# Adaptive layer norm, attention and MLP on one core: priorities varied by kind and time, gates folded into weights, q placed by DMA, two head groups moved

## The chip, the core and the metric

One core of a Trainium2 chip runs the whole program. The metric is device time in microseconds (us), the median over several executions. A profile is one execution taken by the hardware profiler; its span runs from the first to the last instruction. Engines: PE (matrix multiply, with PEld for its weight loads), DVE (VectorE), ACT (ScalarE), POOL (GpSimd), SP (issues DMAs).

## The reference

A transformer block on x of 2048 rows by 512 columns. Six vectors (shift, scale and gate for two branches) come from a conditioning vector c. Cut to what matters:

```python
mod = silu(c) @ w_mod                       # 512 -> 6 x 512: sa, ca, ga, sb, cb, gb
h = layernorm(x) * (1 + ca) + sa
q, k, v = split(h @ wqkv)                   # 32 heads of 16 columns
o = softmax(q @ k.T / 4) @ v                # per head, 2048 x 2048 scores
x = x + ga * (o @ wo)
h = layernorm(x) * (1 + cb) + sb
x = x + gb * (gelu(h @ w1 + b1) @ w2 + b2)  # inner width 1376
```

All tensors are bfloat16. The gates ga and gb are one value per output column.

## The kernel before, in words

**Tiles.** Rows are handled in four blocks b of 512 queries. The 32 heads are four groups cc of eight; a group's q and k lie in 128 partitions, so that four heads (one of each pair, picked by a parity) are multiplied at once in four 32-row strips of PE. A "run" is one block, one group and one parity: 32 runs of 16 key tiles of 128 keys. A score tile is one strip's 128 keys by 512 queries; there are 32 x 16 x 4 = 2048. For the last block a run is both parities and half of the queries.

**q.** `make_q` projects q of a block and group into PSUM and writes the tile `qm` with two halves, one per parity: q scaled, with the rows of the other parity set to zero by the mask `qmask` (L701), so that the 32-row strip's matmul adds only the wanted head of the pair.

**Exponentials on two engines.** Three or two score tiles at a time go to PSUM (`st`) and ACT takes their exponential to `pt` (L840). Of each run up to four key tiles (2, 6, 10, 14) are shared: DVE takes the exponential instead, by an integer trick: one `ph` (L881) per score tile and, for a whole key tile, four shifted copies `sh` (L896), all five summed on PE with weighted copies `VX` of v. If DVE is behind, ACT takes shared tiles as well (`next_tile`, `d_run`). L791 are the score matmuls, L929 the products with v into `od`.

**Normalisation.** At a run's end DVE copies `od` (L954). SP sends the sums to DRAM and back (`dn`, `dc`), DVE inverts them (L965), SP spreads them (`rn`, `RB`), POOL multiplies (L981), and for every second run SP moves the odd heads' rows into place (L991).

**Tails.** `block_tail` follows a block's last run: Wo (L1079), times the gate ga (L1129), plus x (L1131), layer norm, W1 (L1148), bias (L1158), gelu on ACT (L1167), W2 (L1085), times the gate gb (L1180), plus the residual (L1183), out. Its pieces are spread over the next runs. The last block is done in two halves: the first by `block_tail` with two row tiles, the second by `last_half` (L1232, L1237, L1240, L1268, L1271, L1284, L1287), when no scores are left. Of the first half's eleven W1 tiles `PSUM_F` = 4 are taken out by DVE early; the others wait for PSUM that the scores free.

**What sets the order.** The kernel writes its order itself. Each piece of work is an `Op` with an engine, an estimated duration, what it depends on and a priority; `Plan` steps through an estimated time and picks on each engine the ready operation of the lowest priority number (`pick`, `dyn`, `commit`). What it picks is emitted in that order. On the chip every engine takes its instructions in order and waits on semaphores where data is not there. `heat` inserts matmuls without use to keep PE's clock up. All DMAs but one stand in SP's queue. The first loads are, in order: two halves of x's first block, two blocks of w_mod, three 128-column parts of wqkv, then the other blocks of x and the rest of wqkv.

**Order of runs.** `runs` goes block by block, group by group, parity by parity. k and v of a later group are made with a due time before its first run (`due`, `urgent`).

Of the kernel before, what the change touches and what calls it, by code (L numbers as in the profile page):

```python
# [59 lines left out]
FILL = 1.6  # L60
HEAT = 1.3
# [41 lines left out]
class Plan:  # L103
# [39 lines left out]
    def pick(self, eng):  # L143
        can = [(self.start(o), o) for o in self.lists[eng] if o.gate is None or o.gate()]
        can = [(s, o) for s, o in can if s < 1e17]
        if not can:
            return None
        if eng == "PE":
            can = self.ahead(can)
        first = min(s for s, _ in can)  # L150
        near = [(self.dyn(self, o), s, o.seq, o) for s, o in can if s <= first + self.SLACK[eng]]
        _, s, _, o = min(near)
        return s, o

# [22 lines left out]
    def commit(self, s, o):  # L177
# [36 lines left out]
        if o.kb:  # L214
            q = "SP"
            self.bus[q] = max(self.bus[q], s + o.us + 0.9) + o.kb / (310.0 if s < 12.0 else 260.0)
            o.end = self.bus[q] + 0.7
# [33 lines left out]
def kernel(  # L251
# [15 lines left out]
    P = 128  # L267
# [23 lines left out]
    PSUM_F = 4  # L291
# [29 lines left out]
    r_qm = res("qm", 4, [P, 2, QB], BF16)  # L321
# [4 lines left out]
    r_y = res("y", 2, [P, D], BF16)  # L326
# [165 lines left out]
    for h in range(2):  # L492
# [3 lines left out]
    o_wm = {i: dma(lambda o, i=i: nc.sync.dma_start(out=o.tile, in_=wm_src[:, :, i * D:(i + 1) * D]),  # L496
                   kb=512, acq=r_blk, prio=0.01 + 0.01 * i) for i in (0, 1)}
# [4 lines left out]
    def load_cols(i, lo, hi, prio):  # L502
        return dma(lambda o: nc.sync.dma_start(out=o_w[i].tile[:, :, lo:hi],
                                               in_=wq_src[:, :, i * D + lo:i * D + hi]), (o_w[i],),
                   kb=hi - lo, prio=prio)
    o_w0 = {i: load_cols(i, 0, P, 0.1 + 0.01 * i) for i in range(3)}
    o_w1 = {}
    for b in range(1, NQ):
        o_x[b] = load_x(b)
        o_x[b].prio = 0.2 + 0.1 * b  # L510
        o_w1[b - 1] = load_cols((1, 2, 0)[b - 1], P, D, 0.25 + 0.1 * b)
# [16 lines left out]
    o_mask = op("DVE", mask, 0.4, (o_io,), prio=0.0)  # L528
# [163 lines left out]

    def make_q(b, cc, kind, acq):
        qm = op("NIL", None, 0.0, (), lat=0.0, prio=0.0, acq=r_qm)
        mm = proj(b, o_w[0], cc, kind, acq, after=qm)
        if (b, cc) == (0, 0):
            evs = [op("DVE", lambda o, p=p: nc.vector.tensor_scalar(
                out=qm.tile[:, p, :], in0=mm.tile[:, 0:QB], scalar1=qmask[:, p:p + 1], scalar2=None,
                op0=ALU.mult), 0.6, (mm, qm, o_mask), prio=0.1 if p == 0 else 0.45, rel=(mm,)) for p in range(2)]
        else:  # L700
            evs = 2 * [op("DVE", lambda o: nc.vector.tensor_tensor(  # L701
                out=qm.tile, in0=mm.tile[:, 0:QB].unsqueeze(1).to_broadcast([P, 2, QB]),
                in1=qmask.unsqueeze(2).to_broadcast([P, 2, QB]), op=ALU.mult), 1.14, (mm, qm, o_mask),
                prio=0.3, rel=(mm,))]
        o_q[(cc, b)] = (qm, evs)
        qm.uses += 1
        q_left[(cc, b)] = 8 * NT
# [31 lines left out]
    runs = [(b, u) for b in range(NQ) for u in range(8)]  # L739
# [260 lines left out]

    def beside(fn, deps, rel=(), prio=0.5):

        return [op("POOL", lambda o, c=c: after_dve(fn(slice(c * HB, (c + 1) * HB))), POOL_US, deps, lat=0.1,
                   prio=prio, kind="beside", rel=rel, port=True, gate=lambda: plan.beside(POOL_MIN))
                for c in range(2)]
# [66 lines left out]
    def residual(o, ps, gate_t, dst, base, y):  # L1072
        nc.vector.tensor_tensor(out=y, in0=ps, in1=gate_t, op=ALU.mult)
        nc.vector.tensor_tensor(out=dst, in0=y, in1=base, op=ALU.add)

# [39 lines left out]
    def block_tail(b, nt=TPB):  # L1115
# [8 lines left out]
        for t in range(nt):  # L1124
            a = chain([(lambda ps, t=t, u=u: wo_mm(ps, b, t, u, u + 1), MM) for u in range(NC)],
                      [x for u in ots for x in u.two] + [prev], kind, r_ax, ots, 2)
            prev = a
            y = op("NIL", None, 0.0, (a, x2, o_late["ga"]), lat=0.0, prio=0.0, acq=r_y)
            m = op("DVE", lambda o, t=t, a=a, y=y: nc.vector.tensor_tensor(  # L1129
                out=y.tile, in0=a.tile, in1=ga_bc, op=ALU.mult), 0.6, (y,), prio=0.1, rel=(a,))  # L1130
            res_done.append(op("DVE", lambda o, t=t, y=y: nc.vector.tensor_tensor(  # L1131
                out=x2.tile[:, t, :], in0=y.tile, in1=xr.tile[:, t, :], op=ALU.add), 0.33,
                (m, xr), prio=1.5, rel=(y,), port=True))
# [40 lines left out]
        for t in range(nt):  # L1174
# [4 lines left out]
            y = op("NIL", None, 0.0, (mm,), lat=0.0, prio=0.0, acq=r_y)  # L1179
            m = op("DVE", lambda o, mm=mm, y=y: nc.vector.tensor_tensor(  # L1180
                out=y.tile, in0=mm.tile, in1=gb_bc, op=ALU.mult), 0.6, (y,), prio=3.0 if part else 0.1,
                rel=(mm,))
            a = op("DVE", lambda o, t=t, y=y: nc.vector.tensor_tensor(  # L1183
                out=o.tile, in0=y.tile, in1=x2.tile[:, t, :], op=ALU.add), 0.33,
                (m, o_late["gb"]), prio=3.0 if part else 1.5, acq=r_o, rel=(y, x2), port=True)
# [6 lines left out]
    def last_half():  # L1192
# [17 lines left out]
        for n, t in enumerate(tiles):  # L1210
# [18 lines left out]
            def wo2(o, t=t):  # L1229
# [6 lines left out]
            y = take(r_y, (w, x2))  # L1236
            m = op("DVE", lambda o, t=t, y=y: nc.vector.tensor_tensor(  # L1237
                out=y.tile, in0=acc[t].tile, in1=ga_bc, op=ALU.mult), 0.62, (y,), prio=0.024 + n / 50,
                rel=(acc[t],))
            a = op("DVE", lambda o, t=t, y=y: nc.vector.tensor_tensor(  # L1240
                out=x2.tile[:, t, :], in0=y.tile, in1=xr.tile[:, t, :], op=ALU.add), 0.34,
                (m, xr), prio=0.023 + n / 50, rel=(y,))
# [32 lines left out]
            for f in range(NF):  # L1275
# [7 lines left out]
            y = take(r_y, (prev,))  # L1283
            m = op("DVE", lambda o, first=first, y=y: nc.vector.tensor_tensor(  # L1284
                out=y.tile, in0=first.tile, in1=gb_bc, op=ALU.mult), 0.66, (y,), prio=0.1,
                rel=(first,))
            a = op("DVE", lambda o, t=t, y=y: nc.vector.tensor_tensor(  # L1287
                out=o.tile, in0=y.tile, in1=x2.tile[:, t, :], op=ALU.add), 0.34, (m,), prio=0.1,
                acq=r_o, rel=(y,))
# [7 lines left out]
    for b in range(NQ):  # L1297
# [14 lines left out]
        make_v(b, 0, kind, r_ax, "DVE")  # L1312
    for cc in range(1, NC):
        due(32 + APR * (2 * cc - 1) - CB, CB * 0.7 / 8)
# [12 lines left out]
    def want_q(g):  # L1327
        while q_made[0] < g and q_made[0] + 1 < NQ * NC:
            q_made[0] += 1
            b, cc = divmod(q_made[0], NC)  # L1330
# [3 lines left out]
            if cc == NC - 1:  # L1334
                o_h[b].uses -= 1
                if b == NQ - 1:
                    o_w[0].uses -= 1
# [4 lines left out]
    while True:  # L1342
# [7 lines left out]
        while ended:  # L1350
# [4 lines left out]
            for cc in range(1, NC):  # L1355
                if r >= 2 * cc - 3:
                    urgent.add(f"c{cc}")
                    urgent.add(f"in{cc}")
# [4 lines left out]
            if r == 0:  # L1363
                late_loads(o_last[0])
                o_late["ga"] = gate_bc(ga_bc, o_late[2], "gate")
                lt = {3: o_late[3], 4: o_late[4]}
# [16 lines left out]
            if r == 6:  # L1383
# [3 lines left out]
                o_late["w2"] = W2[1]  # L1387
# [39 lines left out]
```

## Time and profile before

| what | us |
|---|---|
| median of 6 runs | 790.29 (788.9 to 791.76) |
| profiled execution | 790.98 |
| its span | 789.2 |
| first exponential starts | 15.48 |
| last exponential ends | 763.7 |
| mean of one exponential, three tiles / two | 1.528 / 1.103 |

The granted TensorE clock is 0.997 over the span. A group's line in the profile reads: line, engine, operation, out<-in with shapes, count, then busy time and the mean ns of one, then the idle time of the engine just before them and what ended it. Durations overlap: an engine starts the next instruction before the last has quite ended, so a sum of durations is above the busy time. In the chain of waits each line is start, length, what.

### The profile page before, as it was taken

Reading aid. Unit: us, or ns where it says so; the run is one execution under the profiler, and the core shown is the slowest. Engines: PE = TensorE matmul, PEld = TensorE weight load, DVE = VectorE, ACT = ScalarE, POOL = GpSimd, SP = SyncE. Lnnn points to the kernel's source line nnn. Section 1 sums busy time; section 2 is a strip of 40 time slices with the busy share of each in tenths; the row PEclk is TensorE's granted clock in tenths of the full one; section 3 lists DMA queues with packets and bytes.
Section 4 is the critical chain, followed back from the end, with each engine's and each line's share of the span. In section 5 each row is a group of like instructions: output and inputs, shape, how many; then the busy total and the mean of one; then the engine's idle time right before and its main releaser. Section 6 shows DMA issues by size and latency. Waiting matters only on the chain.

```text
span 789.2 us, 20172 instructions
## 1 busy us (share of the span) xinstructions
PE 731.2 (93%) x8167; PEld 273.4 (35%) x8249; DVE 742.0 (94%) x1297; ACT 760.6 (96%) x690; POOL 99.0 (13%) x239
## 2 busy tenths in 40 slices
PE   8899999998999999999999999999999999999997
PEld 3433323332323322222322322232233443434444
DVE  6879799999999999999999999999999999999974
ACT  4999999999999999999999999999999999999993
POOL 5622303200001101010001000000000110010000
PEclk9999999999999999999999999999999999999999
DMA  7214000102100000001100000001100001000010
GB/s 214 81 61 107 19 16 19 44 8 68 43 19 15 20 15 20 16 9 31 50 20 16 17 19 2 19 29 30 45 17 20 5 18 44 19 24 15 27 44 27
DMA packets 35231, 26.22 MB, mean 33 GB/s; under 512 B 16037, under 2 KB 30534, under 8 KB 35138
## 3 DMA queue, kind: packets, MB, share of 16 engines
q1 hardware_dynamic: 35130, 24.94, 11.2%
q8 instruction: 64, 1.05, 0.5%
q14 instruction: 29, 0.24, 0.1%
q10 hardware_dynamic: 8, 0.00, 0.0%
HBM read 21.30 MB, written 2.61 MB: 30 GB/s over the span
## 4 chain that ended last, share of the span: by engine, by line
ACT 36%; PE 30%; DVE 19%; issue 11%; DMA 3%; SPq 0%; POOLq 0%; DVEq 0%; POOL 0%; ACTq 0%
ACT pt L840 36%; PE od L929 10%; PE st L791 8%; DVE ph L881 7%; DVE sh L896 6%; PE ax L1085 3%; PE ax L791 2%; PE ax L1148 2%; PE ax L682 1%; DVE g L1158 1%; DVE qm L701 1%; DMA dn<-OD 1%; DMA blk<-in_w_mod_dram 1%; DMA dc<-dn 1%; DVE OD L954 1%
## 5 line engine op out<-in xcount | busy, mean ns | idle before, releaser
L840 ACT ACTIVATE pt<-st 128x1536 bf16<-128x1536 f32 x632 | 718.0, 1316 | 3.7 <-PE st L791 1.9
L881 DVE TENSOR_SCALAR ph<-ax 128x512 int16<-128x512 f32 x468 | 306.6, 685 | 12.4 <-PE ax L791 11.1
L896 DVE TENSOR_SCALAR sh<-ph 128x2048 int16<-128x2048 int16 x468 | 304.6, 693 | 1.4 <-PE od L929 0.9
L791 PE MATMUL st<-qm,kT 32*128 32x512 bf16 x1580 | 247.6, 383 | 27.6 <-ACT pt L840 22.8
L929 PE MATMUL od<-sh,VX 128*32 128x512 bf16 (+1 forms) x2352 | 166.5, 341 | 7.2 <-DVE sh L896 6.2
L791 PE MATMUL ax<-qm,kT 32*128 32x512 bf16 x468 | 162.9, 379 | 4.7 <-DVE ph L881 3.7
L791 PEld LDWEIGHTS <-kT 32*128 32x128 bf16 x2048 | 82.7, 91 | 240.5 <-issue 230.7
L929 PE MATMUL od<-pt,VEB 128*32 128x512 bf16 (+1 forms) x1972 | 147.4, 340 | 0.7 <-ACT pt L840 0.4
L929 PEld LDWEIGHTS <-VEB 128*32 128x32 bf16 x2560 | 62.4, 96 | 78.5 <-issue 66.0
L929 PEld LDWEIGHTS <-VX 128*32 128x32 bf16 x2352 | 58.7, 95 | 87.2 <-issue 75.7
L981 POOL TENSOR_TENSOR OT<-OD,RB 128x256 bf16<-128x256 f32 x38 | 27.5, 736 | 284.3 <-DVE sh L896 189.7
L929 PE MATMUL od<-ph,VEB 128*32 128x512 bf16 (+1 forms) x588 | 46.5, 339 | 1.1 <-DVE OD L954 0.9
L981 POOL TENSOR_TENSOR OS<-OD,RB 128x256 bf16<-128x256 f32 x24 | 17.2, 727 | 187.3 <-DVE sh L896 166.0
L1148 PE MATMUL ax<-blk,W 128*128 128x512 bf16 (+1 forms) x128 | 36.8, 369 | 1.5 <-issue 0.5
L682 PE MATMUL ax<-blk,w 128*128 128x512 bf16 x96 | 33.0, 390 | 3.8 <-DVE blk L607 1.2
L728 POOL TENSOR_SCALAR VX<-VEB 128x128 bf16<-128x128 bf16 x64 | 23.5, 367 | 56.2 <-DVE VEB L614 52.4
L1085 PE MATMUL ax<-w,g 128*128 128x512 bf16 x101 | 28.6, 381 | 0.7 <-issue 0.2
L1158 DVE TENSOR_SCALAR g<-ax,b1c 128x512 bf16<-128x512 f32 (+1 forms) x37 | 26.6, 718 | 0.1
L588 DVE BATCH_NORM_STATS2 ln_s<-xb 128x6 f32<-128x512 bf16 x32 | 21.8, 680 | 1.9 <-DMA xb<-in_A_x_dram 1.8
L954 DVE COPY OD<-od 128x512 f32<-128x512 f32 x31 | 21.3, 686 | 2.4 <-PE od L929 1.6
L1085 PEld LDWEIGHTS <-g 128*128 128x128 bf16 x176 | 14.2, 97 | 21.3 <-issue 11.0
L1148 PEld LDWEIGHTS <-W 128*128 128x128 bf16 x176 | 13.9, 97 | 20.4 <-issue 14.0
(109 smaller groups left out, 364.6 us busy)
## 6 DMA issues: line engine op xcount, KB each, us to landing
RB<-rn SPq DMA_DIRECT2D x124, 64.0 KB
xb<-in_A_x_dram SPq DMA_DIRECT2D x8, 512.0 KB
out_dram<-o SPq DMA_DIRECT2D x16, 128.0 KB
W<-in_B_w_dram SPq DMA_DIRECT2D x1, 1376.0 KB
w<-in_A_wqkv_dram SPq DMA_DIRECT2D x3, 384.0 KB
blk<-in_w_mod_dram SPq DMA_DIRECT2D x2, 512.0 KB
g<-in_w_mod_dram SPq DMA_DIRECT2D x2, 512.0 KB
xb<-in_w_mod_dram SPq DMA_DIRECT2D x2, 512.0 KB
```

The lines of the kernel that those rows point to most:

```text
L682: return chain([(lambda ps, j=j: nc.tensor.matmul(out=ps[:, 0:QB], lhsT=w.tile[:, j, cc * P:(cc + 1) * P], rhs=o_h[b].tile[:, j, :], start ...
L728: nc.gpsimd.tensor_scalar(out=v_cols(VX[(t, ph)])[:, 8 * cc:8 * cc + 8, 0:16], in0=v_cols(v_tile(t, 0))[:, 8 * cc:8 * cc + 8, 0:16], scala ...
L791: nc.tensor.matmul(out=o.tile[:, k * QB:(k + 1) * QB], lhsT=kT[cc][kb][rows, ko * P:(ko + 1) * P], rhs=qm.tile[rows, par, :] if hb is None ...
L840: nc.scalar.activation(out=e.tile[:, 0:len(got) * QB], in_=o.tile[:, 0:len(got) * QB], func=ACT.Exp, scale=ESC)
L881: nc.vector.tensor_scalar(out=ph.tile[:, o.row * QB:(o.row + 1) * QB], in0=o.tile, scalar1=PH_B, scalar2=0.0, op0=ALU.add, op1=ALU.max)
L896: sh = op("DVE", lambda o, j=j: nc.vector.tensor_scalar(out=o.tile, in0=first.tile, scalar1=PH_SH[j], scalar2=None, op0=ALU.add), 0.6, es, ...
L929: nc.tensor.matmul(out=o_od[r].tile[32 * i:32 * i + 32, n * HB:n * HB + w], lhsT=v_tile(kt, ph)[:, c0:c0 + 32], rhs=got[i][:, at:at + w], ...
L954: OD = op("DVE", lambda o: nc.vector.tensor_copy(out=o.tile, in_=od.tile), 0.6, (last,), prio=0.0, acq=r_OD, rel=(od,))
L981: two = beside(lambda c: nc.gpsimd.tensor_tensor(out=OT.tile[:, c], in0=OD.tile[:, c], in1=o5.tile[:, c], op=ALU.mult), (OT,), (OD, o5))
L1085: nc.tensor.matmul(out=ps, lhsT=g[:, f, col:col + P], rhs=rhs, start=(f == 0), stop=(f == NF - 1))
L1148: mm = chain([(lambda ps, f=f, j=j: nc.tensor.matmul(out=ps[:, 0:N], lhsT=W1[:, j, f * P:(f + 1) * P], rhs=h.tile[:, j, 0:N], start=(j == ...
L1158: ev.append(op("DVE", lambda o, f=f, mm=mm: nc.vector.tensor_scalar(out=g.tile[:, f, 0:N], in0=mm.tile[:, 0:N], scalar1=b1c[:, f:f + 1], s ...
```

## The change

- `Plan.pick` adds to every operation's priority a term from 0 to 0.15 (`SPREAD`), a hash of the operation's kind and of a seed; there are 32 seeds, one for each 25 us of planned time.
- The gates are multiplied into weights once, on POOL: ga into Wo and WoP, gb into W2 and W2c (`scaled`, `w2_scaled`; W2c's last row tile holds b2 as well). So the residual of a tile is one DVE operation (PSUM plus x) in place of two (PSUM times gate, plus x). The tile `y` goes.
- q, but for the first group: DVE writes a scaled copy `qs`, and eight DMAs of 16 partitions by 512 columns place its rows in `qm`, whose other rows POOL has zeroed once, at the start.
- Order of runs: after block 0 group 0 come block 1 group 0, block 0 group 1, block 1 group 1, then the rest block by block; the due times of k and v of the later groups follow (`wait`).
- `PSUM_F` goes from 4 to 8: in the first half of the last block DVE takes out eight W1 tiles early, and three are left.
- The first load of wqkv waits until the first block of w_mod has landed (`behind`). Some estimates of durations change.

The instructions that come out differ by these counts: 476 `ph` and 476 `sh` (468 before); 314 exponentials of three tiles and 315 of two (316 each); 15 `qs` for 15 `qm` products; 32 residual operations for 64; 34 more POOL products, six more POOL memsets; 120 more DMAs on SP.

```diff
+SPREAD = 0.15
+SEEDS = (571, 338, 517, 702, ...)
...
-        near = [(self.dyn(self, o), s, o.seq, o) for s, o in can if s <= first + self.SLACK[eng]]
+        near = [(self.dyn(self, o) + self.spread(o), s, o.seq, o) for s, o in can if s <= first + self.SLACK[eng]]
...
+    def spread(self, o):
+        x = ((sum(map(ord, o.kind)) if o.eng == "PE" else o.fn.__code__.co_firstlineno if o.fn else 0) * 2654435761 ^ SEEDS[min(int(self.now // 25.0), len(SEEDS) - 1)] * 2246822519) & 0xFFFFFFFF
+        x = ((x ^ x >> 15) * 2246822519) & 0xFFFFFFFF
+        return SPREAD * ((x ^ x >> 13) & 1023) / 1024.0
...
-    PSUM_F = 4
+    PSUM_F = 8
...
+    QM = [keep.tile([P, 2, QB], BF16, name=f"qm{n}") for n in range(4)]
...
+    def behind(i, load):
+        tc.add_manual_dep(load.ins, first[i].ins.name, mybir.DependencyInfo(
+            mybir.DependencyClass.Sync, mybir.DependencyReason.DATA), reason="order of loads")
...
+            got = nc.sync.dma_start(out=o_w[i].tile[:, :, lo:hi], in_=wq_src[:, :, i * D + lo:i * D + hi])
+            if lo == 0 and i == 0:
+                behind(0, got)
...
+    o_qz = [op("POOL", lambda o, n=n, p=p: nc.gpsimd.memset(QM[n][:, p, :], 0.0), 0.5, prio=0.5 + n)
+            for n in range(1, 4) for p in range(2)]
...
-            evs = 2 * [op("DVE", lambda o: nc.vector.tensor_tensor(
-                out=qm.tile, in0=mm.tile[:, 0:QB].unsqueeze(1).to_broadcast([P, 2, QB]),
-                in1=qmask.unsqueeze(2).to_broadcast([P, 2, QB]), op=ALU.mult), 1.14, (mm, qm, o_mask),
-                prio=0.3, rel=(mm,))]
+            qs = op("DVE", lambda o: nc.vector.tensor_scalar(
+                out=o.tile, in0=mm.tile[:, 0:QB], scalar1=QSC, scalar2=None, op0=ALU.mult), 0.6, (mm, qm),
+                prio=0.3, acq=r_qs, rel=(mm,))
+
+            evs = []
+            for p in range(2):
+                rows = [dma(lambda o, at=slice(i, i + 16), p=p: nc.sync.dma_start(
+                    out=qm.tile[at, p, :], in_=qs.tile[at, :]), [qs] + o_qz, kb=16, n=1.4, prio=0.4 + p, rel=(qs,))
+                    for i in range(16 * p, P, 32)]
+                evs.append(op("NIL", None, 0.0, rows, lat=0.0, prio=0.0))
...
-    runs = [(b, u) for b in range(NQ) for u in range(8)]
+    early = [(1, 0),(0, 1),(1, 1)]
+    groups = [(0, 0)] + early + [(b, cc) for b in range(NQ) for cc in range(NC) if (b, cc) not in [(0, 0)] + early]
+    runs = [(b, 2 * cc + p) for b, cc in groups[:LAST * NC] for p in range(2)] + [(LAST, u) for u in range(8)]
+    wait = {cc: 2 * groups.index((0, cc)) for cc in range(NC)}
...
+    def scaled(parts, gate_t, deps):
+        got = []
+        for w in parts:
+            got += beside(lambda c, w=w: nc.gpsimd.tensor_tensor(
+                out=w()[:, c], in0=w()[:, c], in1=gate_t[:, c], op=ALU.mult), deps, prio=2.0)
+        return op("NIL", None, 0.0, got, lat=0.0, prio=0.0)
...
-            m = op("DVE", lambda o, t=t, a=a, y=y: nc.vector.tensor_tensor(
-                out=y.tile, in0=a.tile, in1=ga_bc, op=ALU.mult), 0.6, (y,), prio=0.1, rel=(a,))
-            res_done.append(op("DVE", lambda o, t=t, y=y: nc.vector.tensor_tensor(
-                out=x2.tile[:, t, :], in0=y.tile, in1=xr.tile[:, t, :], op=ALU.add), 0.33,
-                (m, xr), prio=1.5, rel=(y,), port=True))
+            res_done.append(op("DVE", lambda o, t=t, a=a: nc.vector.tensor_tensor(
+                out=x2.tile[:, t, :], in0=a.tile, in1=xr.tile[:, t, :], op=ALU.add), 0.6,
+                (a, xr), prio=0.1, rel=(a,)))
```

The other three residuals (`block_tail`'s output, both of `last_half`) change in the same way.

## The prediction

> **What bounds the kernel now.** I read the page's busy shares first, then the busy time by stretch, then who waits for whom inside the long stretch, then the chain of waits for the pace of the exponentials, and last the timeline of the first 16 and the last 25 us.
>
> ```profile
> PE 731.2 (93%) x8167; PEld 273.4 (35%) x8249; DVE 742.0 (94%) x1297; ACT 760.6 (96%) x690; POOL 99.0 (13%) x239
> ```
> ```profile
> 0.00:28.00 28.00, 23.15 (x187) 10.81 (x189) 20.87 (x52) 15.12 (x18) 15.14 (x66) 1.00 0.68 207
> 28.00:764.00 736.00, 687.38 (x7809) 249.16 (x7882) 708.24 (x1216) 733.10 (x638) 82.22 (x170) 1.00 0.10 26
> 764.00:789.20 25.20, 20.64 (x181) 13.44 (x178) 12.90 (x30) 12.39 (x36) 1.60 (x4) 0.98 0.14 43
> ```
> The columns behind the stretch's length are PE, PEld, DVE, ACT, POOL. Three engines look nearly full, but from 28 to 764 us only ACT is: 733.1 of 736.0 us, 2.9 us idle, while DVE has 27.8 and PE 48.6 us of idle time. Before 28 us ACT works 15.1 us of 28; behind 764 us half. So there are three stages: a head (until the exponentials run without gaps), a body that lasts as long as ACT's queue of exponentials, and a tail (last query rows through the MLP). What ACT waits for in the body is little:
> ```profile
> ACT pt L840 <- PE ax L791: 1.1, 3, 0.8
> ACT pt L840 <- PE st L791: 0.9, 4, 0.4
> ACT pt L840 <- PE od L929: 0.3, 1, 0.3
> ```
> The pace of ACT is in the chain of waits (start, length, what):
> ```profile
> 84.39 1.21 ACT pt L840
> ...
> 86.62 1.14 ACT pt L840
> ...
> 88.85 1.14 ACT pt L840
> ```
> A pair of exponentials (three score tiles of 512 columns, then two) starts every 2.23 us: 0.446 us a tile. Starts at 82.14, 83.47, 84.39 split that into 1.33 and 0.91.
>
> **The change part by part.** The profiled execution took 790.98 us, its span 789.2; the median of the six runs is 790.29, so differences worked out on this profile are taken off 790.29.
>
> Body, ACT. A score tile that DVE exponentiates is one that ACT needn't. In the instructions that the planner emits, DVE's share rises from 468 to 476 tiles; ACT's falls by two triples and one pair: 2 x 1.33 + 0.91 = 3.6 us. ACT is the bound, so this is worth 3.6 us if nothing makes ACT wait. It needs DVE and PE to keep up:
> ```profile
> L881 DVE TENSOR_SCALAR ph<-ax 128x512 int16<-128x512 f32 x468 | 306.6, 685 | 12.4 <-PE ax L791 11.1
> L896 DVE TENSOR_SCALAR sh<-ph 128x2048 int16<-128x2048 int16 x468 | 304.6, 693 | 1.4 <-PE od L929 0.9
> L701 DVE TENSOR_TENSOR qm<-ax,qmask 128x1024 bf16<-128x1024 f32 x15 | 18.3, 1217 | 1.0 <-PE ax L682 1.0
> L1183 DVE TENSOR_TENSOR o<-y,xb 128x512 bf16<-128x512 bf16 x14 | 6.0, 429 | 0.0
> ```
> A ph of 685 ns recurs every 0.60 us in the chain ("219.04 1.20 DVE ph L881 x2"), so an operation holds DVE some 0.085 us less than its duration. Folding the gates removes 32 second operations like L1183 (the multiply, 0.686 us, becomes the add, also PSUM in): 32 x (0.42 - 0.085) = 10.7 us. The 15 qm products of 1.217 become qs of half the columns (like ph, 0.685): 15 x 0.53 = 8.0. Added: 8 ph and 8 sh, 16 x 0.60 = 9.6; four more 256-wide g evictions in the last block, 4 x 0.39 = 1.6 (0.480 less 0.085). Net 7.5 us less on DVE before contention: it keeps up, and none of it is itself on the path. PE gets 8 more groups of four attention-value matmuls (8 sh and 2 ph more, 2 pt less); the chain has four groups in 0.98 us ("68.19 0.98 PE od L929 x16"), so 2.0 us, less 4 heating groups (1.0 us): hidden in 48.6 us.
>
> GpSimd's 34 new products (gates into Wo, WoP, W2, W2c). Nearest row: L981's 62 products of the same 128x256, 0.73 us each. [...] What contention cost is in DVE's durations:
> ```profile
> L896 DVE TENSOR_SCALAR sh<-ph x468: 629/687/1096, 45.7 to 759.7; 128x2048 int16<-128x2048 int16 x156
> ```
> Median 687, mean 693, longest 1096 ns: 468 x 6 ns = 2.8 us over 62 products, 0.05 us each, so 34 cost 1.5 us of DVE. [...] The products' users (Wo in run 12, W2 later) are runs of 24 us away. Six new memsets of qm (nearest: 0.524, W2c) put 2.1 us ahead of the silu on GpSimd; its result is read by PE at 7.87, 3.8 us after it was ready: cost 0, 2 if that cover were gone.
>
> q by DMA: eight 16 KB DMAs for each of 15 groups on SP's queue, 120 in all. Nearest row: L991's (OT<-OS, same 16 partitions), 0.59 us an issue, one per 0.62. [...] The trace has the issues overlap: dn issued at 601.58, its reader dc at 603.28, so 1.7 us to landing, and eight take 7 x 0.62 + 1.7 = 6.0 us. I take the row. Against it stands how far ahead each q is made. In PE's order of the changed kernel, the last projection matmul and the first score matmul that reads it are 94, 48, 31, 37, 28, 91, 92, 78, 37, 21, 28, 49, 18, 18 and 38 score tiles apart; 2048 tiles take 748 us (15.5 to 763.7), 0.365 us each. The two shortest are 6.6 us, and there the DMAs are issued behind dn, two, dc, four, rn, two. The first score rows need the first and the fifth: 1.2 (PSUM landing, qs) + 0.54 (dn) + 4 x 0.62 + 0.34 (dc) + 1.7 = 6.3 us, just in time; the rows that need the last ones, behind rn, come 3 to 4 us later. A late q stops PE, and behind it every matmul of ACT's next scores; ACT has at most the 2.2 us that two score buffers hold. Price 0 to 2 us at each of the two, 0.5 each taken: +1.0. Behind these issues SP holds RB and OT moves; their readers lie a run away: 0.
>
> Groups moved early and priorities: they move k and v of the second head group from run 2 to run 4, when ACT already runs without gaps; the first block's tail goes from run 8 to run 12. The bound's work is the same: 0, ends -1 and +2 (a reordered PE queue can make ACT wait more than today's 2.9 us).
>
> Head. First exponential at 15.48:
> ```profile
> 2.78 4.37 SPq L503 DMA_DIRECT2D w<-in_A_wqkv_dram  x3
> ...
> 10.00 0.55 PE L564 MATMUL ax<-sc,blk 128*128 128x1 bf16 x16 [0.50 <-DMA blk<-in_w_mod_dram]
> ```
> The second modulation block lands at 10.0 because it shares the engines with the w loads issued from 2.78 on. Now w waits for the first block to land, so the second should land sooner (w's 0.39 MB at 207 GB/s: up to 1.9). But PE and ACT work on: transposes (10.4 to 11.4), DVE and ACT modulation to 13.3, projections. In the new order transposes are split around the second block; I take 0.4 us of gain, ends -1.9 and +1.0 (w or the next x late; w is needed at 11.5).
>
> Tail.
> ```profile
> 768.13 0.43 DVE L1240 TENSOR_TENSOR xb<-y,xb 128x512 bf16<-128x512 bf16 x1 [0.21 <-DMA xb<-in_A_x_dram]
> ...
> 783.34 1.24 PE L1085 MATMUL ax<-w,g 128*128 128x512 bf16 x5
> 783.61 0.69 DVE L1284 TENSOR_TENSOR y<-t,gb_bc 128x512 bf16<-128x512 f32 x1 [1.29 <-PE t L1085]
> 784.34 0.42 DVE L1287 TENSOR_TENSOR o<-y,xb 128x512 bf16<-128x512 bf16 x1
> 784.42 0.81 PE L1085 MATMUL ax<-W2c,g 128*128 128x512 bf16 x3
> 785.27 0.69 DVE L1180 TENSOR_TENSOR y<-ax,gb_bc 128x512 bf16<-128x512 f32 x1 [0.51 <-PE ax L1085]
> 785.99 0.42 DVE L1183 TENSOR_TENSOR o<-y,xb 128x512 bf16<-128x512 bf16 x1
> ```
> PE sets this end: the last eight W2 matmuls (783.34 to 785.2) belong to a tile whose inputs were long ready. With eight instead of four first-layer tiles evicted before the scores end, 16 of the 28 matmuls L1148 in the tail go (0.6 us per four: 2.4 us), and in the new order all of that tile's W2 matmuls stand before the last tile's first layer. Saved behind: 8 x 0.215 = 1.7 us. The last add is gone: 0.42. Against it: the first residual add read x at 768.13 only because x had just landed; the fused one, 0.69 instead of 0.43, starts there too: +0.26. Sum -1.9; ends -2.5 and -0.5 (both output adds now stand before the last tile's residual on DVE).
>
> Sum: -3.6 + 1.0 - 0.4 - 1.9 = -4.9; 790.98 becomes 786.1 in a profile, the median 790.29 becomes 785.4.
>
> **Rivals.** (A) as summed: 785.4. (B) The exponentials' 3.6 us come back as ACT waiting, since PE's queue, at 93%, takes a new order that ACT's pace doesn't fit, or two late q's cost 2 us each; head and tail remain: 790.3 - 0.4 - 1.9 = 788.0, or a little above. For it: PE already waits for ACT's buffers in many places. Against: only 2.3 us of ACT waits now. (C) Slower: q arrives late. SP is served in order, and its waits are
> ```profile
> SPq L970 <- DVE dc L965: 96.2, 29, 7.3
> SPq L962 <- DMA dn<-OD: 34.8, 30, 3.8
> ```
> 3.3 us on average for rn and 1.2 for dn, up to 7.3 and 3.8. Six groups have 31 tiles (11.3 us) or less. If q's DMAs stand behind both waits at twice their mean, 6.3 grows to 6.3 + 1.2 + 6.6 = 14 us; the six would be late by 3 us and more, 1.5 us of it beyond ACT's buffers: 6 x 1.5 = 9 us, 794.4. It decides from 0.9 us per group on. Against: most first rows need only DMAs ahead of rn.
>
> **Chances.** A 0.63, B 0.21, C 0.16. About 0.2% (1.6 us) is what a measurement can tell from no change. Faster: nearly all of A and over half of B, 0.74; within: 0.10; slower: C and a little of B, 0.16. A's range is 782.0 (head -1.9, q 0, tail -2.5: 790.3 - 8.0 = 782.3) to 788; with B to 790.5; what is left out is C and some 0.04 below.
>
> **What would show it.** Right: 629 exponentials; ACT idle in its body still about 3 us; no PE wait for qm DMAs over 1 us; the end of the exponentials some 4 us earlier; tail 23 us instead of 25. Wrong: PE waiting for "DMA qm<-qs" for many us, sh's mean well over 700 ns, or ACT idle over 6 us in the body.

## The result, and the profile after

The changed kernel takes 788.93 us (median of 33 runs, 785.9 to 793.55); the kernel before took 790.64 in the 68 runs beside it. The ratio is 0.9976, 95% interval 0.9965 to 0.9987: faster by 1.7 us, where 4.9 had been forecast. The profiled execution took 787.92 us, its span 786.1.

Three parts of the profile answer to those shown of before. The page's busy times and the rows of VectorE's two exponential operations:
```profile
PE 731.0 (93%) x8209; PEld 272.3 (35%) x8286; DVE 737.4 (94%) x1285; ACT 757.3 (96%) x683; POOL 125.2 (16%) x279
...
L912 DVE TENSOR_SCALAR ph<-ax 128x512 int16<-128x512 f32 x476 | 312.2, 684 | 11.8 <-PE ax L822 10.3
L927 DVE TENSOR_SCALAR sh<-ph 128x2048 int16<-128x2048 int16 x476 | 312.0, 696 | 2.6 <-PE od L960 2.3
```
The busy time by stretch (columns as before: length, PE, PEld, DVE, ACT, POOL, granted clock):
```profile
0.00:28.00 28.00, 23.25 (x191) 11.46 (x193) 19.97 (x52) 15.58 (x18) 18.30 (x75) 1.00 0.55 169
28.00:764.00 736.00, 690.54 (x7875) 250.63 (x7947) 708.57 (x1214) 732.29 (x637) 105.28 (x201) 1.00 0.11 30
```
What ACT waits for between 28 and 764 us:
```profile
ACT pt L871 <- PE st L822: 1.4, 4, 0.6
ACT pt L871 <- PE ax L822: 1.4, 3, 0.9
```
ACT has less to do (757.3 us for 760.6, three exponentials fewer). Between 28 and 764 us it is idle 3.7 us (736.00 less 732.29) where it was idle 2.9, and the waits that carry its name are hardly more than before. So the stages themselves were measured:

| | before | after |
|---|---|---|
| first exponential starts | 15.48 | 15.07 |
| last exponential ends | 763.73 | 761.46 |
| from there to the end (the tail) | 25.44 | 24.69 |
| the exponentials' own pitch (their count times 1.33 or 0.904 us) | 705.0 | 701.5 |
| what their starts come later than that pitch, summed | 14.1 | 16.1 |

The last row is needed because most late starts are too short to be listed as waits: 60 or 100 ns here, 1.25 us there. It is the sum, over all exponentials, of the distance to ACT's next start less 1.33 (three tiles) or 0.904 us (two). It is called *lateness* below.

One more column is needed to compare kernels. Each run lists the mean TensorE clock that was granted in it, and the time follows it along a line: in 33 runs of the changed kernel 0.48 us for each 0.001. Read from such a line, fitted to each kernel's own runs, at a clock of 1.0 ("at full clock"), before is 788.8 to 789.2 (five groups of 12 to 51 runs), after 787.0. So some 2.0 us are gained at full clock. The mean clocks, 0.9955 after and 0.9964 before, make 0.45 us the other way, but that is chance as far as these runs tell: the five groups of the kernel before have 0.9951 to 0.9973 among themselves. A reading at full clock from 6 or 12 runs near it is good to some 0.6 us.

### The profile page after: what moved, and what is told of

Its sections match the earlier page's. It is cut to its first block, busy times and chain, and to the rows that moved or that the text cites. A ratio compares the mean times of both kernels' runs of the same rounds, so it can differ in the third digit from the quotient of the medians.

```text
span 786.1 us, 20448 instructions
## 1 busy us (share of the span) xinstructions
PE 731.0 (93%) x8209; PEld 272.3 (35%) x8286; DVE 737.4 (94%) x1285; ACT 757.3 (96%) x683; POOL 125.2 (16%) x279
## 4 chain that ended last, share of the span: by engine, by line
ACT 23%; PE 21%; DVE 12%; issue 8%; DMA 2%; SPq 0%; POOL 0%; POOLq 0%; DVEq 0%; ACTq 0%
ACT pt L871 21%; PE od L960 7%; PE st L822 6%; DVE sh L927 4%; DVE ph L912 4%; PE ax L1123 3%; PE ax L1183 2%; PE ax L822 1%; ACT g L1202 1%; DVE ln_s L607 1%; DMA qm<-qs 1%; DVE xb L1166 1%; PE t L1123 1%; DMA xb<-in_A_x_dram 1%; DVE OD L985 0%
## 5 line engine op out<-in xcount | busy, mean ns | idle before, releaser
L912 DVE TENSOR_SCALAR ph<-ax 128x512 int16<-128x512 f32 x476 | 312.2, 684 | 11.8 <-PE ax L822 10.3
L927 DVE TENSOR_SCALAR sh<-ph 128x2048 int16<-128x2048 int16 x476 | 312.0, 696 | 2.6 <-PE od L960 2.3
L822 PE MATMUL ax<-qm,kT 32*128 32x512 bf16 x476 | 167.3, 379 | 8.2 <-DVE ph L912 6.1
L960 PE MATMUL od<-sh,VX 128*32 128x512 bf16 (+1 forms) x2400 | 168.6, 342 | 5.9 <-DVE sh L927 4.8
L822 PEld LDWEIGHTS <-kT 32*128 32x128 bf16 x2048 | 80.8, 91 | 239.9 <-issue 230.5
L960 PE MATMUL od<-pt,VEB 128*32 128x512 bf16 (+1 forms) x1960 | 144.6, 341 | 0.3 <-ACT pt L871 0.3
L960 PEld LDWEIGHTS <-VX 128*32 128x32 bf16 x2400 | 60.7, 95 | 87.2 <-issue 76.5
L1183 PE MATMUL ax<-blk,W 128*128 128x512 bf16 (+1 forms) x145 | 39.7, 358 | 1.8 <-issue 0.6
L756 POOL TENSOR_SCALAR VX<-VEB 128x128 bf16<-128x128 bf16 x64 | 23.1, 360 | 80.8 <-DVE VEB L633 77.0
L1193 DVE TENSOR_SCALAR g<-ax,b1c 128x512 bf16<-128x512 f32 (+1 forms) x41 | 28.3, 695 | 1.0 <-PE ax L1183 0.7
```

Of the source, the lines that this page charges most:

```text
L756: nc.gpsimd.tensor_scalar(out=v_cols(VX[(t, ph)])[:, 8 * cc:8 * cc + 8, 0:16], in0=v_cols(v_tile(t, 0))[:, 8 * cc:8 * cc + 8, 0:16], scala ...
L822: nc.tensor.matmul(out=o.tile[:, k * QB:(k + 1) * QB], lhsT=kT[cc][kb][rows, ko * P:(ko + 1) * P], rhs=qm.tile[rows, par, :] if hb is None ...
L912: nc.vector.tensor_scalar(out=ph.tile[:, o.row * QB:(o.row + 1) * QB], in0=o.tile, scalar1=PH_B, scalar2=0.0, op0=ALU.add, op1=ALU.max)
L927: sh = op("DVE", lambda o, j=j: nc.vector.tensor_scalar(out=o.tile, in0=first.tile, scalar1=PH_SH[j], scalar2=None, op0=ALU.add), 0.6, es, ...
L960: nc.tensor.matmul(out=o_od[r].tile[32 * i:32 * i + 32, n * HB:n * HB + w], lhsT=v_tile(kt, ph)[:, c0:c0 + 32], rhs=got[i][:, at:at + w], ...
L1183: mm = chain([(lambda ps, f=f, j=j: nc.tensor.matmul(out=ps[:, 0:N], lhsT=W1[:, j, f * P:(f + 1) * P], rhs=h.tile[:, j, 0:N], start=(j == ...
```

## The experiments

Labels beginning with a_ edit the changed kernel, b_ the kernel before. "Order held" means that each engine's instructions stand in the changed kernel's order but for what the edit names. This is not so by itself: the seeded term hashes the line number of the code behind an operation, so that a line inserted above can reorder everything.

**Tail: the late load of x.** The first residual of the last rows (L1267) waits, and the chain of waits of the changed kernel leads through x:
```profile
762.51 0.59 SPq L1022
763.10 0.04 issue
763.15 3.95 DMA xb<-in_A_x_dram
```
Its timeline has both ends of that, and PE's matmuls for the same residual, which were done at 765.8:
```profile
760.67 2.43 SPq L1022 DMA_DIRECT2D OT<-OT  x4
...
763.15 0.58 SPq L491 DMA_DIRECT2D xb<-in_A_x_dram  x1
...
765.22 0.59 PE L1263 MATMUL t<-WoP,OT 128*128 128x512 bf16 x2
...
767.22 0.69 DVE L1267 TENSOR_TENSOR xb<-t,xb 128x512 bf16<-128x512 f32 x1 [3.59 <-DMA xb<-in_A_x_dram]
```
The load stands on SP behind four moves of OT rows, and those begin 0.79 us before the exponentials end, where before they began 2.01 us ahead of it:
```profile
759.95 1.74 POOL L981 TENSOR_TENSOR OT<-OD,RB 128x256 bf16<-128x256 f32 x2 [18.57 <-DVE sh L896]
...
761.72 2.42 SPq L991 DMA_DIRECT2D OT<-OT  x4
...
764.19 0.58 SPq L483 DMA_DIRECT2D xb<-in_A_x_dram  x1
```
x landed 5.6 us after the exponentials' end instead of 4.3. The moves wait for GpSimd's last products, and in the changed kernel those stand behind VectorE's L1193, the bias of the W1 tiles that it takes out early:
```profile
759.23 1.42 POOL L1012 TENSOR_TENSOR OT<-OD,RB 128x256 bf16<-128x256 f32 x2 [18.09 <-DVE g L1193]
```

a_xearly and b_xearly load x two runs earlier, in either kernel:
```diff
+            if r == NR - 3:
+                state["x"] = load_x(LAST)
...
-        xr = load_x(b)
+        xr = state["x"]
```


> The changed kernel, with x of the last 256 query rows' block loaded two runs earlier, when SP has nothing ahead of it; the planned order of every engine up to the last run is the same. Theory (the late x load, issued at 763.15 behind the four moves of OT rows and landing at 767.10, holds the first residual of the tail 1.3 us and eats most of the tail's saving): 1.0 to 1.5 us faster than the changed kernel's 788.9, so 787.4 to 787.9, and the wait of the fused residual (3.59 us for the x load) is gone from the timeline; the tail is 23.2 to 23.7 us instead of 24.7. Rival (the tail is set by PE's matmuls and the layer norm's steps all the same, so the wait is passed on): under 0.3 us, 788.6 to 788.9.

> The kernel before, with the same edit. There the residual waited only 0.21 us for x and the multiplication by the gate ran ahead of it, so both theories expect at most 0.2 us: 790.4 to 790.7. If it gains 1 us or more here too, the early load is a gain of its own, and no explanation of what the change lost.

Measured: a_xearly 788.3 us (ratio 0.997, 0.9955 to 0.9986), 786.1 at full clock; b_xearly 790.25 (0.9999, 0.9984 to 1.0014), tail 25.47. Before gains nothing (there, too, the planner moved a few operations of the tail). In the changed kernel the residual starts 1.34 us sooner after the exponentials' end, but the tail is only 0.75 shorter (23.94): the planner had moved the last output addition and a W2 matmul behind everything. a_xheld takes that away: only the DMA moves.

> The changed kernel with one DMA moved: the load of x for the last 256 query rows is issued two runs earlier; every other instruction keeps its place on its engine (in the earlier try the planner had also moved the last output addition behind everything). Theory (the late load costs what it delayed the tail's first residual by, 1.34 us against the end of the exponentials): 1.3 us faster than the changed kernel's 788.9, so 787.6; the tail 23.3 us. Rival (something else in the tail comes up in its place): 0.6 us or less.

Measured: 786.77 (ratio 0.9941, 0.9919 to 0.9964), tail 23.42, 785.25 at full clock. Later it was run again:

> The same kernel as the one with only x's DMA moved early, again: 785.3 at full clock, and a median that follows from the clock at about 0.5 us per 0.001: 786.8 at 0.9978, 787.6 at the changed kernel's 0.9955.

Measured: 786.85 (ratio 0.995, 0.993 to 0.9969) at a mean clock of 0.9971, 785.5 at full clock, tail 23.42. In its timeline the residual starts 0.1 us after PE's two matmuls for it end (the label names ACT's g, which ends within 0.1 us of them, but the residual reads only t and xb):
```profile
765.52 0.59 PE L1264 MATMUL t<-WoP,OT 128*128 128x512 bf16 x2
...
766.21 0.69 DVE L1268 TENSOR_TENSOR xb<-t,xb 128x512 bf16<-128x512 f32 x1 [2.25 <-ACT g L1189]
```
One DMA issued too late cost 1.3 us of tail. The version with it moved is faster than both kernels, at full clock by 0.9 to 1.7 us against the changed one, as the line is taken (the medians, 2.1 us apart, have a difference of clock in them).

**Tail: the eight W2 matmuls.** a_psum4 and a_psum4x set `PSUM_F` back to 4, with x late and with x early.

> The changed kernel with four instead of eight first-layer tiles taken out before the scores end; the planned order differs only in the last runs. The prediction put this part of the tail at 1.7 us (eight second-layer matmuls out of the end): 790.6, with the tail 26.4 us instead of 24.7. Rival (the x load that lands late set the tail already, and the matmuls that moved forward only filled the wait): under 0.7 us, 788.9 to 789.6.

> The changed kernel with x of the last rows loaded early (as in the run where only that DMA was moved) and four instead of eight first-layer tiles taken out early. Theory (with x late the saving of the tail only filled the wait; with x early it shows): 1.4 to 1.7 us slower than the run with x early alone (785.25 at full clock), so about 786.8 at full clock, and the tail 25 us instead of 23.42. Rival (the term of 1.7 us was wrong by itself): within 0.5 us, tail 23.9 or less.

Measured: a_psum4 788.69 us, tail 24.97, so 0.28 us above the changed kernel's; a_psum4x 788.8 us, tail 24.80, so 1.38 above x early alone, and 787.15 at full clock, 1.6 to 1.9 above it. With x early the theory held: the term of 1.7 us is right in size. With the load in its old place the rival's number came, but not as it was put, for in a_psum4 x is not late:
```profile
757.23 1.74 POOL L1012 TENSOR_TENSOR OT<-OD,RB 128x256 bf16<-128x256 f32 x2 [16.30 <-DVE sh L927]
...
759.00 2.42 SPq L1022 DMA_DIRECT2D OT<-OT  x4
...
761.47 0.58 SPq L491 DMA_DIRECT2D xb<-in_A_x_dram  x1
...
765.17 0.69 DVE L1267 TENSOR_TENSOR xb<-t,xb 128x512 bf16<-128x512 f32 x1 [1.93 <-PE t L1183]
```
The exponentials end at 761.08 there, so the moves begin 2.08 us ahead of it, as in the kernel before, and the residual waits for PE. So `PSUM_F` = 8 itself makes x late: with eight tiles to take out, GpSimd's products come behind VectorE's L1193, the moves behind the products, the load behind the moves. It takes 1.4 to 1.6 us of matmuls off the tail and adds 1.3 us of waiting for x.

**Body: q by DMA.** a_qheld lets the `qs` operation write the masked product of 1024 columns into `qm`, and issues no DMA.

> The changed kernel in the same planned order, but q is written by one masked VectorE product of 1024 columns straight into its place, as before the change, and the 120 DMAs are not issued. Theory (q by DMA costs PE under 1 us in all, 0.7 us of waits in the trace): 0 to 1 us faster, 788.0 to 788.9; VectorE is busy 8 us more, hidden. Rival (what the body lacks, about 2 us of exponentials that start late, comes from late q's): 2 us faster, 787 or below, and the late exponentials fall by as much.

Measured: 793.07 us (ratio 1.0021, 1.0008 to 1.0035), 790.2 at full clock: 3.3 us slower. Neither theory. VectorE is given 8.0 us by count (15 operations of 1217 instead of 686 ns), 7.2 by the page's busy time (744.6 for 737.4), and nearly half of it comes through. Lateness rises from 16.1 to 20.9; about 1.6 of that is a second stretch at half clock in this profile (see below).

Where q did come late, a_xearly's timeline shows it best: the last two of its DMAs stand on SP behind rn, and PE waits for them; ACT's next exponential was 1.72 us late (0.76 in the changed kernel's own profile, 0.87 and 0.92 in those of a_xheld and a_xheld2).
```profile
582.74 0.25 DVE L996 RECIPROCAL dc<-dc 128x16 f32<-128x16 f32 x1
...
583.48 1.85 SPq L1001 DMA_DIRECT2D rn<-dc  x1
...
585.42 1.14 SPq L729 DMA_DIRECT2D qm<-qs  x2
586.06 0.37 PE L822 MATMUL ax<-qm,kT 32*128 32x512 bf16 x1 [1.26 <-DMA qm<-qs]
```
rn did not wait for the reciprocal here: that had ended at 582.99, and rn's issue began at 583.48, 0.05 us behind the DMA ahead of it. But this one issue took 1.85 us. In the other three profiles rn's took 0.58, and the q DMA right behind it 1.26 to 1.42 in place of some 0.55. The profile's inferred label for rn's extra 1.3 us is VectorE's `sh`, which rn does not read; why an issue takes longer there is not settled.

Two attempts to mend the lateness, both made in the belief that the wait for the reciprocal causes it, and both with x early and the other engines' order held. a_xq8 issues all eight at the first one's place; a_xqrn only moves those directly behind rn to directly ahead of it.

> The changed kernel with x of the last rows loaded early, and with the eight DMAs of each q issued one after the other at the place of the first, so that none stands behind the wait for the reciprocals on SP; all other engines keep their order. Theory (the late exponential at 585 us, 0.76 us in one profile of the changed kernel and 1.72 in another, is q's last DMAs behind that wait, and it is the only such place): 0.6 to 1.5 us faster than x early alone, 784.2 at full clock, and no PE wait for q's DMAs. Rival (the exponentials of the next key tiles come late for other reasons all the same, or the normalisation now comes late behind q): within 0.3 us, 785.2, or slower.

> The changed kernel with x of the last rows early, and with those DMAs of q that stood on SP directly behind the wait for the reciprocals (one or two in eleven groups) issued directly ahead of it; everything that stood ahead of them keeps its place, and so does every other engine. Theory (their lateness makes the late exponential at 585 us, 0.76 and 1.72 us in two profiles): 0.5 to 1 us faster than x early alone at full clock (785.25), so 784.2 to 784.8, and no PE wait for q's DMAs. Rival (x early alone shows no such wait in its own profile, so it comes only in some executions): within 0.3 us of it.

Measured: a_xq8 833.75 us, 47 us slower than x early alone; some 16 of them go with the clock, 0.963. The DMAs now stand ahead of dc, dc lands later, and the reciprocal that reads it holds VectorE's whole queue. The same row of the waits, of the changed kernel and of a_xq8:
```profile
DVE dc L996 <- DMA dc<-dn: 2.1, 3, 1.4
```
```profile
DVE dc L996 <- DMA dc<-dn: 35.3, 13, 4.4
```
a_xqrn: 790.47 us, 787.6 at full clock, 2 us slower than x early alone. The late exponential at 585 is gone, but the one after that at 605.9 comes 2.21 us late, behind a PE wait for the next group, whose remaining six DMAs were issued in one go:
```profile
602.63 3.67 SPq L1435 DMA_DIRECT2D qm<-qs  x6
606.39 0.53 SPq L1001 DMA_DIRECT2D rn<-dc  x1
```
```profile
607.68 0.37 PE L822 MATMUL ax<-qm,kT 32*128 32x512 bf16 x1 [1.64 <-DMA qm<-qs]
```
Without the edit (a_xheld2) PE read that q at 607.02 with no wait. Why it then waits for the last of the six wasn't settled. So the planner's place for q's DMAs was the better one, and q's lateness is about what the prediction had put it at.

**Body: gates.** a_gateheld writes each residual as two operations again, in the place of the one, and leaves the GpSimd products away; a_gate2 does the same with the planner told; a_nopool leaves the products out and puts nothing in their place.

> The changed kernel in the same planned order, but gates are not folded: GpSimd's 34 products are not issued, and each residual is two VectorE operations again (multiply, then add), back to back in the place of the one. Theory (the products cost next to nothing; VectorE's 10.7 us are hidden in the body, only the last add of 0.42 us and the 0.3 us or so of the tail's first residuals show): 0.4 to 1.5 us slower, 789.3 to 790.4. Rival (the products block VectorE and make the body late): 1 us faster or more, 787.9 or below, with a mean of the four-shift operation under 690 ns instead of 696.

> The changed kernel without the folded gates (no GpSimd products, two VectorE operations for each residual), with the planner told of their length, so that it orders the work anew. It gives VectorE 468 of the score tiles instead of 476. Theory (the planner turns VectorE time into tiles at 0.446 us of ACT each, and the exponentials' end is the sum of ACT's tiles): 8 tiles x 0.446 = 3.6 us, and 0.7 us of the tail's second additions: 793.2. Rival (VectorE's time is the bound in any order, and the extra 10.7 us show as they did when the order was held): 799 or more. Third (VectorE's extra work is hidden in its idle time, as the prediction had it): 789.6.

> The changed kernel in the same order with GpSimd's 34 products of gate and weight left out, and nothing in their place, so the gates are not applied. Theory (contention cost 1.5 us of VectorE, and VectorE is not as idle as it looked): 0 to 1 us faster, 787.9 to 788.9; the four-shift operation's mean 693 instead of 696. [...]

Measured: a_gateheld 803.49 us, at full clock 797.3 (798.3 if the changed kernel's 0.48 us for each 0.001 is taken, since no run lay near 1.0): 10.3 to 11.3 us, for 10.7 us of VectorE work by the forecast's count and 12.9 by the page's busy time (750.3 for 737.4). VectorE's idle time took in 2.6 us at most. a_gate2 takes 804.15, no better, but in another order, with eight tiles fewer on VectorE and a tail of 28.8 us. What ACT waits for in a_gateheld (28 to 761 us), against 1.4 and 1.4 us in the changed kernel:
```profile
ACT pt L871 <- PE st L822: 5.8, 10, 0.9
ACT pt L871 <- PE ax L822: 5.6, 10, 1.3
...
PE ax L822 <- DVE ph L912: 8.6, 30, 1.1
PE od L960 <- DVE sh L927: 8.4, 24, 0.9
```
PE waits for VectorE, ACT for PE, in the runs in which a block's tail is worked in. a_nopool: 789.92 us, at full clock 787.5 against 787.0: nothing gained beyond what such readings scatter. Its mean `sh` is 692 ns, as in other profiles that have the products (692 and 694 in a_xheld and a_xheld2). The products cost nothing that can be seen. In the changed kernel's profile 30 of the 34 begin while VectorE reads PSUM. The one that began 0.02 us behind an `sh`, at 127.51, took 1187 ns where the median of the 34 is 672. Five `sh` began before a product had ended: three took 782 to 839 ns, two 695 and 725, where the 419 that no operation of GpSimd overlaps take 683 on average.

**Body: the order.** Four kernels planned anew: q on VectorE with the planner told, the seeded term at 0, other seeds, the runs in the old order.

> The changed kernel with q written by one masked VectorE product again, with the planner told, so that it orders anew. VectorE gets 456 tiles instead of 476. Theory (tiles at 0.446 us of ACT): 20 x 0.446 = 8.9 us, less up to 1 us of waits for q's DMAs: 796.8 to 797.8. Rival (q by DMA brings late exponentials of 2 us or more, which go): 795 or below. Third (what VectorE saves is hidden): 788 to 789.

> The changed kernel with the seeded term of the priorities at 0; all else is as changed. VectorE gets 464 tiles instead of 476. Theory (tiles): 12 x 0.446 = 5.4 us: 794.3. Rival (the seeded term only brings disorder on PE and late exponentials): 788 or below. If neither: the difference beyond 5.4 us is what the order itself is worth.

> The changed kernel with 32 other seeds (each old one times 7 plus 13, modulo 1000). VectorE gets 468 tiles. Theory (the seeds are worth the tiles that their order lets VectorE take): 8 x 0.446 = 3.6 us: 792.5. Rival (any seeds do, tiles or not): within 1 us of 788.9. Third (order luck apart from tiles): more than 2 us off 792.5.

> The changed kernel with the runs block by block as before the change (no head groups moved early), planned anew. VectorE gets 460 tiles instead of 476. Theory (tiles at 0.446 us): 16 x 0.446 = 7.1 us slower, 796.0, plus or minus what another order is worth; the seeds fit the one order that they came with. Rival (the moved groups matter for nothing, as the prediction took them): 788 to 790.

| | tiles on VectorE | own pitch, us | lateness, us | mean clock | median, us |
|---|---|---|---|---|---|
| before | 468 | 705.0 | 14.1 | 0.9964 | 790.64 |
| after | 476 | 701.5 | 16.1 | 0.9955 | 788.93 |
| a_qdve | 456 | 710.4 | 12.8 | 0.9961 | 794.56 |
| a_heatheld (below) | 464 | 707.3 | 17.9 | 0.9942 | 795.57 |
| a_seeds2 | 468 | 705.0 | 20.9 | 0.9860 | 796.34 |
| a_order | 460 | 708.2 | 17.3 | 0.9947 | 796.65 |
| a_nospread | 464 | 707.3 | 23.1 | 0.9850 | 800.92 |
| a_gate2 | 468 | 705.0 | 25.7 | 0.9852 | 804.15 |

The ratios' intervals to before are 1.0036 to 1.0078 (a_qdve), 1.0062 to 1.0114 (a_seeds2), 1.005 to 1.0094 (a_order) and 1.0114 to 1.0174 (a_nospread). Tiles at 0.446 us explain the pitch within half a microsecond; what lies beyond is lateness and clock, and depends on the order. In four other orders (a_nospread, a_seeds2, a_order, a_heatheld) nearly the same work is 6.6 to 12.0 us slower than in the changed kernel's, and slower than the kernel before. Pitch makes 3.5 to 6.7 us of it; in a_nospread and a_seeds2 the lower clock goes with another 5 by the line above. The seeded term is worth 12 us against none, 7.4 against the one other set of seeds that was tried. a_order, planned anew with the same seeds, tests another order, and not the moved groups alone.

**Body: the clock.** In these profiles the granted clock falls to 0.5 for 3.41 us at a time. In the changed kernel's profile this happened once in the body (129.2 to 132.6); ACT's starts around it were 1.25 and 0.41 us late, 1.66 of its 16.1 us. The stretches of 3.4 us ahead of it and of the dip itself:
```profile
125.80:129.20 3.40, 2.62 (x40) 1.42 (x44) 3.37 (x10) 3.40 (x5) 2.36 (x3) 1.00 0.07 21
129.20:132.60 3.40, 3.40 (x31) 0.78 (x23) 1.06 (x3) 2.50 (x3) 2.21 (x5) 0.50 0.00 0
```
Two kernels add heating matmuls:
```diff
-            if o.extra:
+            if o.extra or (left[r] > 1 and not first and sum(us for at, us in plan.done if at > plan.now - WIN) < 1.55):
                 zeros(r)
```


> The changed kernel in the same order, with 31 more groups of four heating matmuls, put behind attention-value groups wherever the plan has less than 1.55 us of full-array work in the last 3.4 us (the planner isn't told). Theory (the stretches of 3.41 us at half clock come after 3.41 us with little array work, 0.8 to 1.4 us of it in the traces, and each costs about 1 us): the mean clock rises from 0.9955 to 0.998 or more and the median falls by about 1 us, to 788 or below, in spite of up to 8 us more matmuls. Rival (PE has no room; each group of 0.25 us delays scores): the clock rises, but the time is 1 to 4 us longer. Third (the dips have another cause): the clock stays at 0.9955.

> The changed kernel with every engine's order held, and a group of four heating matmuls more behind those attention-value groups where the plan has less than 1.55 us of full-array work in the last 3.4 us; the planner isn't told. Theory (stretches of 3.41 us at half clock follow windows with little array work): the mean clock rises from 0.9955 to 0.998 or more, the median falls by about 1 us, to 788 or below. Rival (PE has no room): the clock rises, the time at full clock grows by 1 us or more. Third: the clock stays at 0.9955.

Measured: a_heatheld 795.57 us; the line inserted at the top of its code had changed all hashes, it is one more other order and tests nothing of its own. a_heat2 held the order: its mean clock is 0.9972, short of the 0.998 of the theory and hardly above a_xheld2's 0.9971 without the extra matmuls, so it is not shown that they raise it. At full clock it takes 788.4, 1.4 us more, and the median is 789.78. That fits the rival, that PE has no room for them, without proving it.

## Why the prediction was wrong

The direction was right, the size under half. By its own steps, with the lateness of undisturbed bodies (before in b_xearly's profile 13.05; the changed order in a_xheld, a_xheld2 and a_psum4x 14.6, 15.2 and 15.7):

| step | forecast | measured |
|---|---|---|
| three exponentials fewer, at their pitch | -3.6 | -3.56 |
| q late + order and priorities | +1.0 + 0 | +1.5 to +2.6 lateness |
| head | -0.4 | -0.4 (15.48 to 15.07) |
| tail | -1.9 | -0.76 |
| clock | not in the sum | +0.45 (within its scatter) |
| sum | -4.9 | about -2.2; median -1.7 |

- **The tail: the step that failed most plainly.** "The fused one ... starts there too: +0.26" took x's landing as fixed relative to the exponentials' end. It came 1.3 us later, since the moves ahead of it on SP came later, and they came later through the very part that was to shorten the tail: the eight early W1 tiles. With the load moved the tail is 23.42 us, 2.0 shorter than before, and forecast: "tail 23 us instead of 25"; at full clock the gain is then 3.3 to 3.9 us. The prediction had looked at what the load delays, and not at what is queued ahead of it in the changed order.
- **"Groups moved early and priorities: ... 0, ends -1 and +2."** Wrong as a way of thinking. The order is the largest term of all: 6.6 to 12.0 us between it and four others with nearly the same work. The net was small because the order at hand is the best of those tried; that was luck as far as the prediction goes, which gave no reason for it. What this order costs beside before's, up to 1.6 us beyond q's share, was inside the ends.
- **"It keeps up, and none of it is itself on the path" (VectorE).** The balance of work was right, the conclusion not: VectorE's idle 27.8 us did not take work in. Work added in the order held came through by four fifths or more (gates, 10.3 us or more of 12.9 busy) and by nearly half (q, 3.3 of 7.2). So what the fold and q by DMA take off VectorE counts, and is not "hidden". The sum of its work was off too: its busy time fell by 4.6 us (742.0 to 737.4), not by 7.5 less 1.5.
- **q by DMA, +1.0 at two short places.** Right in place and size: one of the two short places, 585 us, 0.76 to 1.72 us late in four profiles; the other shows no wait for q in the changed kernel. Rival C, q late by 9 us, didn't happen. (Its sum takes dn's wait at its mean where it says twice: 15.3 us, not 14; six groups late by 2.7 us, less the 2.2 that ACT's buffers hold, would be 0.5 us each and not 1.5.) But the price of 0 for what stands behind q's DMAs on SP holds only for the places they have: all eight ahead of dc made VectorE wait 35.3 us.
- **GpSimd's products.** 1.5 us of VectorE expected, in a sum that is off the path; no cost seen. In the changed kernel's trace an `sh` that an operation of GpSimd overlaps takes 792 ns on average (57 of them; 683 for the other 419), but only six of the 34 products overlap one; 28 begin beside a `ph`, and a `ph` takes 682 ns where an operation of GpSimd overlaps it and 685 where none does.
- **Rival B** (788.0 or a little above) came nearest in number, but as put it is half right: of the 3.6 us of exponentials 1.5 to 2.6 came back as lateness, and its tail, -1.9, fell short as A's did. ACT's idle time, the sign that was to tell them apart, hardly shows it: 3.7 us, and the lateness grew by 2.0.
- **The clock** was not in the sum at all. The profile of before that the working was based on lay at 0.997 and held one dip in its body (337.5 us), behind a gelu that hid part of it.

What stays open: about 0.5 us between the table's sum and the median, within what the full-clock readings of one kernel scatter (788.8 to 789.2); why PE waited for the last of six DMAs in a_xqrn; why one issue among q's takes 1.3 to 1.9 us; and which part of the lateness beyond q's belongs to which part of the new order.

## What to carry to other kernels

An engine's summed idle time is no room (VectorE's 27.4 us in the changed kernel's body took in at most 2.6 of 12.9 us of added work): ask what a longer instruction delays at its place in the queue, and if in doubt hold the order and make it longer. For a load near the end (x's cost 1.3 us of tail here), look at what stands ahead of it in its queue and when that is released, not only at who reads it; another part of the same change can move the release. When a change lets a scheduler order the work anew, the order itself is a term of the sum (6.6 to 12.0 us between the orders tried here), and its size must be estimated from other orders, not set to 0.

## What the runs showed of the hardware

In the traces of both kernels the granted clock goes to 0.50 for 3.413 us: from 129.18 to 132.60 us in the changed kernel's, from 337.53 to 340.94 in the other's. The changes of the clock lie whole multiples of that length apart (36, 1 and 192 in the changed kernel's trace; 97, 1 and 131 in the other's), so on a grid; counted from the span's start, its first line is at 2.89 us in the one and at 3.02 us in the other. In 19 profiles (all but a_xq8's), 29 stretches at half clock began between 18 and 750 us; 28 of them came after a stretch of the grid in which matmuls did at most 1.4 us of full-array work (a matmul on a quarter of the array counted as a quarter, from the listed matmuls), where the median stretch has 2.0. So little work was not enough by itself: over 150 other stretches had as little and no dip followed. A dip of one such length takes 0.0022 of the mean clock, about 1.05 us by the line above; the changed kernel's 33 runs, from 785.9 to 793.55 us, follow their clock with a correlation of -0.94. Ahead of the changed kernel's dip PE was busy 2.62 of 3.40 us, but of its 40 matmuls 17 were on quarters of the array and 17 had a single column.
